# Windowed attention and two-layer MLP on one core: means of v per head pair in the first chunk, and a listed order for its first operations

## The chip, the cores and the metric

The kernel runs on one core of one Trainium2 chip. The metric is device time in microseconds, from the first to the last instruction with what lies around them; the median of three runs is given, and one execution was taken with a profile. TensorE multiplies matrices, VectorE and ScalarE work on 128 partitions side by side, GpSimd does a little of the same more slowly, and SyncE (SP) starts the transfers between HBM and the core's memory, SBUF.

## The reference

q, k and v are (4, 8, 768, 64): 4 batches, 8 heads, 768 positions, 64 features.

```python
k_sum = k.reshape(B, H, nb, 32, D).max(axis=3)
v_sum = v.reshape(B, H, nb, 32, D).mean(axis=3)
scores_l = scale * (q @ k.T), masked to |i - j| < 16
scores_s = scale * (q @ k_sum.T) + log(32)
a = exp(scores_all - max); a = a / (sum(a) + 1e-9)
out = a @ concat(v, v_sum)
h = x @ w_in                     # x: 3072 x 512, w_in: 512 x 2048
return maximum(0.01 * h, h) @ w_out
```

Every position sees its window of 31 neighbours and 24 block columns (maximum of k, mean of v over 32 positions). x is the attention output of all heads side by side. All is fp32.

## The kernel before, in words

The 3072 tokens are cut into 8 chunks of 384 (`NCH`), each with 4 head pairs (`NP`) and 3 tiles of 128 tokens to a pair: 12 units to a chunk (`UPC`). A unit's attention is this chain: scores on TensorE (`scores`, tiles s0 and s1 for the two heads), one VectorE operation that adds the mask, writes the result to e and its minimum to m (`lowest`), the exponential on ScalarE with its sum in z (`expo`), a guard (z + 1e-9), a reciprocal and the product e times 1/z on VectorE (`guard`, `rec`, `nrm`), a transpose on TensorE into t and its copy pt on ScalarE, the value product o on TensorE (`values`), and the copy of o into x on ScalarE with what the rounding left on VectorE (`xhi`, `xlo`). In the first chunk each unit does this on its own (`unit`); in the second, two units go together (`pair`, groups "g" in the names); later four.

A unit's 120 keys lie in one tile k: for each of 6 half tiles 96 window columns, copied from kn by ScalarE (`windows`), and 24 block columns, copied from ksum by VectorE (`k_s`); ksum is VectorE's maximum over kn (`k_max`). The values lie likewise in v: 96 rows per half tile from HBM, and 24 rows of means. For batch 0 the means come from TensorE: `v_mean_pe` loads all of v of batch 0 as three tiles of 512 KB (vb) and multiplies six pieces with a small averaging matrix that stands behind the mask, into 24 x 512 numbers; ScalarE copies these to vs0, and GpSimd copies them into the v tile of each of the four pairs.

The MLP takes a chunk's x in 16 blocks f of 128 hidden columns: 12 matmuls into h (three products of split numbers for four pieces of 128 features), an activation into gs and ghi on ScalarE, their difference glo on VectorE, and 9 matmuls into three accumulators a0 to a2. The first block's 12 matmuls are split in 9 and 3 (`CUT`), the 9 needing the units of three head pairs only. Its weights arrive as 512 KB tiles (w) of f 0, 1, ... for each of the two matrices and are split on the chip (`weights`): two steps on ScalarE, three on VectorE, of 512 columns each. Chunk 0 runs f 0 to 9, then chunk 1 all 16, then chunk 0 the rest; behind them the later batches go through a scheme with fewer multiplications, which the change does not touch.

What runs when is decided while the program is built. Every operation gets an engine, a cost and a due time (`prio`), and `Plan.order` lists them: the engine that is free first takes, of the operations that are ready by the planner's own clock, the one with the lowest due time. The `LOADS` list gives the first transfers in order. Every engine then executes its operations strictly in that order, and so does SP with the transfers. In gaps that the planner expects on TensorE it puts spare matmuls of zeros (L1343, tile `spare`) until the MLP has begun. Buffers are rings: q, k tiles have two (`KR`), v tiles three (`VR`), so the load of the fourth v tile waits for the first one's value products.

## Time and profile before

| | us |
|---|---|
| median of 3 runs (610.81 to 611.47) | 611.4 |
| span of the profiled execution | 610.0 |
| TensorE busy | 603.5 (99%) |
| VectorE busy | 470.8 (77%) |
| ScalarE busy | 351.2 (58%) |
| GpSimd busy | 4.5 (1%) |
| moved by DMA | 129.99 MB, 213 GB/s |

The span is what lies between the first and the last instruction; the median of the runs stands 1.4 us above it. A matmul's recorded end is modelled and overlaps the next one's start, so a busy TensorE isn't one at its peak, and the spare matmuls count as busy too; what an instruction costs in a dense queue is the distance between two starts. An idle time in brackets is that of the engine in front of the instruction, with what ended it.

### The profile page before, as it was taken

To read this page: it belongs to the slowest core of one execution; us is meant where nothing else is said; L and a number is where in the kernel's file an instruction comes from. 1 tells how busy PE (TensorE), PEld (TensorE's weight loads), DVE (VectorE), ACT (ScalarE), POOL (GpSimd) and SP (SyncE) were. 2 spreads that over 40 slices of the span, in tenths; PEclk is the share of its full clock that TensorE was granted. 3 is DMA by queue.
4 is the path that set the end of the run, shared out by engine and by line. 5 is a ranking of instruction groups with operands and counts; after the bars stand their busy time and mean duration, and the time that the engine had idled before them with its cause. 6 is when DMAs were issued, how large, how long until landed. Compare 5 with 4: busy or idle time off the path is not lost.

```text
span 610.0 us, 12907 instructions
## 1 busy us (share of the span) xinstructions
PE 603.5 (99%) x4676; PEld 539.8 (88%) x4676; DVE 470.8 (77%) x1281; ACT 351.2 (58%) x965; POOL 4.5 (1%) x10
## 2 busy tenths in 40 slices
PE   8999999999999999999999999999999999999997
PEld 6588889889988889989898897989889899999996
DVE  5899999964889995625688884777987874878787
ACT  5899996653766676505567565762816353516060
POOL 0200000000000000000000000000000000000000
PEclk9999999999999999999999999999999999999999
DMA  8897998896868826517498582975848384747552
GB/s 285 251 301 240 298 301 251 264 328 196 272 218 268 258 77 186 187 43 212 115 273 247 159 245 75 280 247 174 299 157 256 119 250 153 237 147 239 155 156 104
DMA packets 83358, 129.99 MB, mean 213 GB/s; under 512 B 7072, under 2 KB 51424, under 8 KB 83296
## 3 DMA queue, kind: packets, MB, share of 16 engines
q1 hardware_dynamic: 83296, 129.18, 68.1%
q8 instruction: 37, 0.61, 0.4%
q14 instruction: 25, 0.20, 0.1%
HBM read 97.72 MB, written 29.36 MB: 208 GB/s over the span
## 4 chain that ended last, share of the span: by engine, by line
PE 88%; DVE 6%; ACT 3%; DMA 1%; issue 1%; SPq 0%; DVEq 0%
PE L L1229 19%; PE h L724 12%; PE X L1090 7%; PE W L1090 7%; PE Z L1090 7%; PE B_a L1040 4%; PE a L744 4%; PE a L745 4%; PE a L743 4%; PE Y L1090 4%; PE B_s L1040 2%; ACT e L383 1%; PE B_to L1040 1%; PE vps L284 1%; DMA big<-in_k_dram 1%
## 5 line engine op out<-in xcount | busy, mean ns | idle before, releaser
L724 PE MATMUL h<-x,win_hi 128*128 128x384 f32 x320 | 82.7, 339 | 0.0
L383 ACT ACTIVATE e<-e,m 128x120 f32<-128x120 f32 x192 | 73.6, 387 | 4.0 <-DVE m L376 3.9
L1229 PE MATMUL L<-wout_hi,win_hi 128*128 128x512 f32 x168 | 66.5, 396 | 0.0
L1229 PE MATMUL L<-wout_hi,win_lo 128*128 128x512 f32 x168 | 65.7, 391 | 0.0
L1229 PE MATMUL L<-wout_lo,win_hi 128*128 128x512 f32 x168 | 65.6, 391 | 0.0
L724 PEld LDWEIGHTS h<-x,win_hi 128*128 128x128 f32 x320 | 57.7, 188 | 2.3 <-issue 0.2
L724 PE MATMUL h<-x,win_lo 128*128 128x384 f32 x160 | 53.8, 336 | 0.0
L743 PE MATMUL a<-wout_hi,ghi 128*128 128x512 f32 x120 | 48.4, 403 | 0.0
L745 PE MATMUL a<-wout_hi,glo 128*128 128x512 f32 x120 | 47.3, 394 | 0.0
L744 PE MATMUL a<-wout_lo,ghi 128*128 128x512 f32 x120 | 47.1, 392 | 0.1
L1229 PEld LDWEIGHTS L<-wout_hi,win_lo 128*128 128x128 f32 x168 | 31.5, 188 | 6.7
L1229 PEld LDWEIGHTS L<-wout_hi,win_hi 128*128 128x128 f32 x168 | 31.6, 188 | 5.8
L1229 PEld LDWEIGHTS L<-wout_lo,win_hi 128*128 128x128 f32 x168 | 31.6, 188 | 5.7
L383 ACT ACTIVATION_READ_ACCUMULATOR e<-e,m 128x1 f32 x192 | 36.4, 190 | 0.0
L734 DVE TENSOR_TENSOR glo<-gs,ghi 128x384 fp32r<-128x384 f32 x40 | 22.1, 554 | 17.1 <-ACT gs L728 16.4
L731 ACT ACTIVATE ghi<-h 128x384 fp32r<-128x384 f32 x40 | 19.4, 486 | 26.7 <-PE h L724 26.6
L1186 ACT COPY P<-X 128x384 f32<-128x384 f32 x19 | 9.0, 473 | 37.0 <-PE X L1090 36.9
L724 PEld LDWEIGHTS h<-x,win_lo 128*128 128x128 f32 x160 | 30.0, 188 | 0.0
L315 ACT COPY k<-big 128x288 f32<-128x288 f32 x64 | 24.7, 433 | 4.5 <-DMA big<-in_k_dram 4.5
L745 PEld LDWEIGHTS a<-wout_hi,glo 128*128 128x128 f32 x120 | 22.5, 188 | 5.4 <-DVE glo L734 0.4
L744 PEld LDWEIGHTS a<-wout_lo,ghi 128*128 128x128 f32 x120 | 22.6, 188 | 3.9 <-DVE wout_lo L693 0.4
L743 PEld LDWEIGHTS a<-wout_hi,ghi 128*128 128x128 f32 x120 | 22.6, 188 | 3.4
(630 smaller groups left out, 1626.0 us busy)
## 6 DMA issues: line engine op xcount, KB each, us to landing
win_hi<-sums SPq DMA_DIRECT2D x73, 256.0 KB
win_lo<-sums SPq DMA_DIRECT2D x71, 256.0 KB
big<-in_w_dram SPq DMA_DIRECT2D x32, 512.0 KB
sums<-big SPq DMA_DIRECT2D x32, 512.0 KB
v<-in_v_dram SPq DMA_DIRECT2D x32, 288.0 KB
big<-in_k_dram SPq DMA_DIRECT2D x16, 400.0 KB
k<-in_q_dram SPq DMA_DIRECT2D x32, 192.0 KB
wout_hi<-sums SPq DMA_DIRECT2D x21, 256.0 KB
```

What stands on the lines that cost most here:

```text
L315: nc.scalar.copy(k, x)
L383: nc.scalar.activation(out=e[:, n], in_=e[:, n], func=AF.Exp, scale=-1.0, bias=m[:, n:n + 1], accum_out=z[:, n:n + 1])
L724: nc.tensor.matmul(h[:, :T], w[:, 512 * f + 128 * k:512 * f + 128 * k + 128], x[:, T * k:T * k + T], start=n == 0, stop=n == 11)
L731: nc.scalar.activation(out=gnew(tag, G("ghi", f)), in_=tl[G("h", f)][:, :T], func=AF.Prelu, alpha=0.01)
L734: nc.vector.tensor_tensor(out=gnew(tag, G("glo", f)), in0=tl[G("gs", f)], in1=tl[G("ghi", f)].bitcast(F32), op=ALU.subtract)
L743: nc.tensor.matmul(o, gh, wout_hi[:, f], start=f == f0, stop=False)
L744: nc.tensor.matmul(o, gh, wout_lo[:, f], start=False, stop=False)
L745: nc.tensor.matmul(o, gl, wout_hi[:, f], start=False, stop=f == f1 - 1)
L1040: nc.tensor.matmul(o[:, x:x + 256], g, w[l], start=fresh and m == 0, stop=m == 5, skip_group_check=True)
L1090: nc.tensor.matmul(o[:, :T], w[:, l, 128 * k:128 * k + 128], x[y][:, T * k:T * k + T], start=start and n == 0, stop=n == 5, skip_group_che ...
L1186: nc.scalar.copy(tmp(K("P1")), ps("X"))
L1229: nc.tensor.matmul(o, g, w[:, f], start=s + m == 0, stop=s == 1 and m == 5)
```

## The change

In the first chunk the means of v are computed per head pair p. `v_mean_pe(p, ...)` makes the 24 x 128 means of one pair from 9 matmuls of 128 columns: six on the v tile of the pair, which is loaded anyway and holds the first half of the positions in overlapping bands (`band`), and three on a tile of 192 KB with the second half (`mm`). They go to partitions 96 to 119 of the bank that the spare matmuls use, which now write partitions 0 to 63. ScalarE copies 128 columns per pair; GpSimd copies into the v tile as before. In all tiles the block columns now stand behind the 96 window columns, and the scale of the scores is applied in the copies into the k tile. In the first chunk the guard is an activation with a bias on ScalarE, the product e times 1/z is one VectorE operation per head with a scalar per partition, and the block-max copies run on GpSimd. The k columns of pair 2 lie in a buffer of their own, so that its load needs no ring place. The order of 580 early operations is written out as a list (`FIRST`, numbers of the operations as they are made) that goes ahead of the due times; `LOADS` is listed anew, and due times and rates of the planner have other values.

```diff
+FIRST = [
+    1, 9, 0, 13, 12, 3, 26, 30, 2, 29, 10, 312, 11, 25, 5, 504, 43, 518, 505, ...
...
+        rank = {n: (-1000.0 + 0.001 * i, n) for i, n in enumerate(FIRST)}
...
-            o = min((x for x in cand[e] if x["ready"] <= t), key=lambda x: (x["prio"], x["n"]))
+            o = min((x for x in cand[e] if x["ready"] <= t), key=lambda x: rank.get(x["n"], (x["prio"], x["n"])))
...
-LOADS = [('kn', 0, 0), ('q', 0, 1), ('q', 0, 0), ('kn', 0, 1), ('mask',), ('vb', 0, 0), ...
+LOADS = [('kn', 0, 0), ('q', 0, 0), ('mask',), ('vb', 0, 0), ('v', 0, 0), ('kn', 0, 1), ...
...
-    def v_mean_pe(t):
-        def load(j):
-            x = bigs(("vb", 0, j))
-            nc.sync.dma_start(out=x.rearrange("p (t d) -> p t d", t=2), in_=a["v0"][j])
...
-            nc.tensor.matmul(tl["vps",][:NS], mask[:, 3 * LK + 20 - 4 * n:3 * LK + 44 - 4 * n], tl["vb", 0, j][:, 512 * i:512 * i + 512],
+    def v_mean_pe(p, t, ahead):
+        key, kv = ("vb", 0, p), ("v", 0, p)
+        half = NT // 2
+        def load():
+            nc.sync.dma_start(out=new("out", key, [128, 512], bufs=TPC)[:, :128 * half], in_=a["v0"][p])
+        def band(n):
+            nc.tensor.matmul(spare[96:LK, 128 * p:128 * p + 128], mask[:96, 3 * LK + 54 - 2 * n:3 * LK + 78 - 2 * n], tl[kv][:96, n], start=n == 0, stop=False)
+        def mm(n):
+            w = 3 * LK + 20 - 4 * (half + n)
+            nc.tensor.matmul(spare[96:LK, 128 * p:128 * p + 128], mask[:, w:w + NS], tl[key][:, 128 * n:128 * n + 128], start=False, stop=n == half - 1)
...
-            nc.scalar.copy(tl["vsum", 0], tl["vps",][:NS])
+            nc.scalar.copy(tl["vs0",][96:LK, 128 * p:128 * p + 128], spare[96:LK, 128 * p:128 * p + 128])
...
-            nc.scalar.copy(k, x)
+            nc.scalar.mul(k, x, -1.0 / math.sqrt(D))
...
-            nc.vector.tensor_copy(k, tl["ksum", b, p].unsqueeze(1).broadcast_to([128, 2 * TPC, NS]))
+            (nc.vector if c or not KSP else nc.gpsimd).tensor_scalar(out=k, in0=tl["ksum", b, p].unsqueeze(1).broadcast_to([128, 2 * TPC, NS]), scalar1=-1.0 / math.sqrt(D), scalar2=None, op0=ALU.mult)
...
         def guard():
             z = tiles_of(m)[2][:, part]
-            nc.vector.tensor_scalar(out=z, in0=z, scalar1=1e-9, scalar2=None, op0=ALU.add)
+            nc.scalar.activation(out=z, in_=z, func=AF.Identity, bias=tiny)
...
-            nc.vector.tensor_tensor(out=e[:, part], in0=e[:, part], in1=z[:, part].unsqueeze(2).broadcast_to([128, 2, LK]), op=ALU.mult)
+            nc.vector.tensor_scalar(out=e[:, n], in0=e[:, n], scalar1=z[:, n:n + 1], scalar2=None, op0=ALU.mult)
...
-                    nc.tensor.matmul(spare[:, :128], zero[:, :128], zero[:, :128], start=True, stop=True)
+                    nc.tensor.matmul(spare[:64, :128], zero[:, :64], zero[:, :128], start=True, stop=True)
```

How the queues stand. First SP's queue of transfers from its beginning, before; big holds kn, vb and w tiles, and in_v0 is the copy of v for the means:

```order
L244 DMA big_87<-in_k_dram 128x800
L310 DMA k_0_1_102<-in_q_dram 128x384
L310 DMA k_0_0_104<-in_q_dram 128x384
L244 DMA big_87<-in_k_dram 128x800
L230 DMA mask_78<-in_mask_dram 128x404
L278 DMA big_87<-in_v0_dram 128x1024
L244 DMA big_87<-in_k_dram 128x800
L278 DMA big_87<-in_v0_dram 128x1024
L310 DMA k_0_2_233<-in_q_dram 128x384
L278 DMA big_87<-in_v0_dram 128x1024
L244 DMA big_87<-in_k_dram 128x800
L672 DMA big_87<-in_w_dram 128x1024
```

And after:

```order
L278 DMA big_87<-in_k_dram 128x800
L361 DMA k_0_0_104<-in_q_dram 128x384
L264 DMA mask_78<-in_mask_dram 128x438
L314 DMA vb_0_0_107<-in_v0_dram 128x384
L370 DMA v_0_0_109<-in_v_dram 96x768
L278 DMA big_87<-in_k_dram 128x800
L361 DMA k_0_1_112<-in_q_dram 128x384
L314 DMA vb_0_1_114<-in_v0_dram 128x384
L370 DMA v_0_1_118<-in_v_dram 96x768
L728 DMA big_87<-in_w_dram 128x1024
L278 DMA big_87<-in_k_dram 128x800
L361 DMA k_0_2_174<-in_q_dram 128x384
```

Pair 0's q, mask, vb and v stand directly behind its kn, and the same four of pair 1 follow; w of f 0 moved from twelfth to tenth place, the first v from thirteenth to fifth.

TensorE's queue around the scores of units 6 to 8 (t is a transpose, vps the means, o a value product), before:

```order
L371 MATMUL s0_6_341<-k_0_2_233 64x120 x2
L371 MATMUL s1_6_342<-k_0_2_233 64x120 x2
L371 MATMUL s0_7_349<-k_0_2_233 64x120 x2
L371 MATMUL s1_7_350<-k_0_2_233 64x120 x2
L284 MATMUL vps_249<-big_87,mask_78 24x512
L371 MATMUL s0_8_369<-k_0_2_233 64x120 x2
L371 MATMUL s1_8_370<-k_0_2_233 64x120 x2
L284 MATMUL vps_249<-big_87,mask_78 24x512
L388 MATMUL t_4_387<-ident_77,e_2_300 120x128 x2
L284 MATMUL vps_249<-big_87,mask_78 24x512 x2
```

And after, where the means are written to spare:

```order
L448 MATMUL o_1_335<-pt_0_271,v_0_0_109 64x64 x4
L448 MATMUL o_0_343<-pt_0_271,v_0_0_109 64x64 x4
L442 MATMUL t_4_351<-ident_77,e_2_283 120x128 x2
L425 MATMUL s0_6_356<-big_87,k_0_2_174 64x120 x2
L425 MATMUL s1_6_357<-big_87,k_0_2_174 64x120 x2
L317 MATMUL spare_100<-v_0_2_191,mask_78 24x128
L425 MATMUL s0_7_372<-big_87,k_0_2_174 64x120 x2
L425 MATMUL s1_7_373<-big_87,k_0_2_174 64x120 x2
L317 MATMUL spare_100<-v_0_2_191,mask_78 24x128 x5
L321 MATMUL spare_100<-vb_0_2_186,mask_78 24x128 x2
L448 MATMUL o_2_401<-pt_1_315,v_0_0_109 64x64 x4
L321 MATMUL spare_100<-vb_0_2_186,mask_78 24x128
```

Three value products (o_1, o_0, o_2) stand ahead of or between these scores now; before, the first one, o_0, stands 59 rows behind the piece shown, with 29 spare matmuls between. In all, 103 spare matmuls stood between the first scores and the last part of h_0_0, and 52 stand there now.

ScalarE's queue around the first weight step (big 128x512, the tile of f 0), before:

```order
L383 ACTIVATE e_3_356,z_3_358<-e_3_356,m_3_357 128x120 x4
L684 ACTIVATE big_87<-big_87 128x512
L289 COPY vs0_399<-vps_249 24x512
L690 CAST win_hi_73<-big_87 128x512
L445 CAST x0_80<-o_0_435 128x128
L439 COPY pt_2_446<-t_4_387 120x256
L445 CAST x0_80<-o_1_440 128x128
L315 COPY k_0_3_297<-big_87 128x3x96 x2
L445 CAST x0_80<-o_2_456 128x128
```

And after (z is the guard):

```order
L474 ACTIVATE z_1_212<-z_1_212,tiny_98 128x2
L437 ACTIVATE e_2_283,z_2_285<-e_2_283,m_2_284 128x120
L740 ACTIVATE big_87<-big_87 128x512
L437 ACTIVATE e_2_283,z_2_285<-e_2_283,m_2_284 128x120
L326 COPY vs0_312<-spare_100 24x128
L474 ACTIVATE z_2_285<-z_2_285,tiny_98 128x2
L494 COPY pt_1_315<-t_2_302 120x256
L746 CAST win_hi_73<-big_87 128x512
L366 ACTIVATE big_87<-big_87 128x3x96
L494 COPY pt_1_315<-t_3_325 120x256
L366 ACTIVATE big_87<-big_87 128x3x96
L437 ACTIVATE e_2_283,z_2_285<-e_2_283,m_2_284 128x120
```

The weight step stands ahead of three of the four exponentials of units 4 and 5, where before it stood behind those of unit 7; the copies of the means, 24x128 instead of 24x512, follow it directly. Ahead of the last x cast of the chunk there stood 6 weight steps before, and 9 now.

## Rows read from the trace of the kernel before

**Rows 1.** Busy us of each engine by stretch (instructions), granted clock, DMA share, GB/s

```profile
0.00:8.00 8.00, 6.89 (x99) 6.46 (x99) 2.01 (x4) 2.76 (x5) 0.70 (x6) 1.00 0.77 250
8.00:16.00 8.00, 7.37 (x80) 4.10 (x81) 6.04 (x41) 6.25 (x28) 0.00 (x0) 1.00 0.94 326
16.00:24.00 8.00, 7.61 (x78) 3.73 (x76) 6.68 (x26) 5.57 (x20) 2.93 (x3) 1.00 0.89 206
60.00:80.00 20.00, 20.00 (x170) 17.20 (x170) 19.74 (x56) 18.99 (x49) 0.00 (x0) 1.00 0.91 296
```

**Rows 2.** Chain of waits behind 56 us: start us, us, what it ran on

```profile
57.65 2.11 PE h L724 x12
...
579.01 1.05 PE Z L1090 x6
```

**Rows 3.** Timeline of TensorE: start us, us, line, operation, tiles, count

```profile
5.90 0.64 PE L371 MATMUL s<-k 64*64 64x120 f32 x16
...
18.49 1.90 PE L284 MATMUL vps<-big,mask 128*24 128x512 f32 x4
20.32 1.79 PE L1343 MATMUL spare<-zero 128*128 128x128 bf16 x29
22.05 0.69 PE L394 MATMUL o<-pt,v 120*64 120x64 f32 x16
...
24.77 0.44 PE L371 MATMUL s<-k 64*64 64x120 f32 x8
25.13 0.45 PE L394 MATMUL o<-pt,v 120*64 120x64 f32 x8
25.51 0.43 PE L388 MATMUL t<-ident,e 128*120 128x128 f32 x2
25.88 0.45 PE L394 MATMUL o<-pt,v 120*64 120x64 f32 x8
...
34.91 0.63 PE L724 MATMUL h<-x,win_hi 128*128 128x384 f32 x2
...
53.38 0.32 PE L371 MATMUL s_('g', 9, 1)_943<-k 64*64 64x120 f32 x2
```

**Rows 4.** Timeline of ScalarE, first 41 us (in brackets idle us before, and releaser)

```profile
3.83 0.77 ACT L315 COPY k<-big 128x288 f32<-128x288 f32 x2 [1.81 <-DMA big<-in_k_dram]
...
19.77 0.70 ACT L684 ACTIVATE big<-big 128x512 f32<-128x512 f32 x1 [1.49 <-DMA big<-in_w_dram]
...
27.31 0.35 ACT L439 COPY pt<-t 120x256 f32<-120x256 f32 x1
27.56 0.44 ACT L315 COPY k<-big 128x288 f32<-128x288 f32 x1
27.89 0.27 ACT L445 CAST x<-o 128x128 fp32r<-128x128 f32 x1
28.05 0.41 ACT L383 ACTIVATE e<-e,m 128x120 f32<-128x120 f32 x1
28.34 0.20 ACT L383 ACTIVATION_READ_ACCUMULATOR e<-e,m 128x1 f32 x1
28.44 0.27 ACT L445 CAST x<-o 128x128 fp32r<-128x128 f32 x1
...
34.45 0.27 ACT L445 CAST x<-o 128x128 fp32r<-128x128 f32 x1
...
40.01 0.68 ACT L690 CAST win_hi<-big 128x512 fp32r<-128x512 f32 x1
40.60 0.70 ACT L684 ACTIVATE big<-big 128x512 f32<-128x512 f32 x1
```

**Rows 5.** Timelines of GpSimd and of VectorE, 21 to 35 us

```profile
21.06 2.93 POOL L327 COPY v<-vs 24x768 f32<-24x768 f32 x3 [19.76 <-ACT vs L289]
...
22.07 1.24 DVE L693 TENSOR_TENSOR win_lo<-big,win_hi 128x512 fp32r<-128x512 f32 x1 [0.75 <-ACT win_hi L690]
...
33.74 0.68 DVE L693 TENSOR_TENSOR win_lo<-big,win_hi 128x512 fp32r<-128x512 f32 x1
```

More of the change, by code (lines that the diff above doesn't have):

```diff
@@ L82, in __init__, with op @@
         self.ops, self.rings, self.users, self.slot = [], {}, {}, {}
-    def op(self, eng, cost, prio, fn, after=(), use=(), alloc=(), size=0, rate=250.0, port=False):
+    def op(self, eng, cost, prio, fn, after=(), use=(), alloc=(), size=0, rate=275.0, port=False):
         o = {"eng": eng, "cost": cost, "prio": prio, "fn": fn, "after": list(after), "size": size, "rate": rate, "n": len(self.ops)}
@@ L184, in build @@
     ident = cst.tile([128, 128], F32, name="ident")
-    mask = cst.tile([128, 3 * LK + 44], F32, name="mask")
+    mask = cst.tile([128, MW], F32, name="mask")
     def gap(n, src, tag):
@@ L201, in build @@
     make_identity(nc, ident)
+    zero = cst.tile([128, 128], BF16, name="zero")
+    nc.vector.memset(zero, 0.0)
+    tiny = cst.tile([128, 1], F32, name="tiny")
+    nc.vector.memset(tiny, 1e-9)
+    spare = ps_acc.tile([128, 512], F32, tag="a2", name="spare")
     def win(n, at, size):
@@ L247, in red @@
             x = tl["kn", b * CPB, p][:, WIN:WIN + S].rearrange("p (n r) -> p n r", r=BLK)
[L248 to L249 removed]
+            (nc.gpsimd if pooled else nc.vector).tensor_reduce(out=new("ksum", ("ksum", b, p), [128, NS], bufs=5), in_=x, axis=AX.X, op=ALU.max)
+        key, pooled = ("kn", b * CPB, p), b == 0 and p in KPOOL
         kn_op[key] = load_op(key, t - 1.3 - ahead, load, after=gate(b), alloc=[("big", key, 0)], size=128 * (S + 2 * WIN) * 4)
[L251 to L253 removed]
+        ksum_op[b, p] = P.op("POOL" if pooled else "DVE", POOL(S) if pooled else DVE(S), t, red, after=[kn_op[key]], use=[key], alloc=[("ksum", ("ksum", b, p), 5)])
+    vs_ops, vs_last = {b: [] for b in range(B)}, []
     def v_mean(b, j, t, ahead):
@@ new lines, in v_mean_pe @@
+    def v_mean_pe(p, t, ahead):
[8 more added lines that the diff above has]
+            nc.tensor.matmul(spare[96:LK, 128 * p:128 * p + 128], mask[:, w:w + NS], tl[key][:, 128 * n:128 * n + 128], start=False, stop=n == half - 1)
+        def copy():
+            if p == 0:
+                new("out", ("vs0",), [128, 512], bufs=TPC)
+            nc.scalar.copy(tl["vs0",][96:LK, 128 * p:128 * p + 128], spare[96:LK, 128 * p:128 * p + 128])
+        lv = v_op[0, p][0]
+        o = load_op(key, t - 1.5 - ahead, load, alloc=[("out", key, TPC)], size=128 * 128 * half * 4)
+        x = vs_last[:]
+        for n in range(2 * TPC):
+            y = P.op("PE", 225, t + 0.01 * n, lambda n=n: band(n), after=[lv, mask_op], use=[kv] + ([("vps",)] if p + n else []), alloc=[] if p + n else [("a2", ("vps",), 1)])
+            y["behind"], x = x and x[0], [y]
+        for n in range(half):
+            y = P.op("PE", 225, t + 0.1 + 0.01 * n, lambda n=n: mm(n), after=[o], use=[key, ("vps",)])
+            y["behind"], x = x[0], [y]
+        vs_last[:] = x
+        o = x[0]
+        vsum_op[0, p] = P.op("ACT", ACT(128, True), t + 0.1, copy, after=[o], use=[("vps",), ("vs0",)] if p else [("vps",)], alloc=[] if p else [("out", ("vs0",), TPC)])
@@ L1330, in build @@
         first[y]["behind"] = first[x]
-        first[y]["prio"] = first[x]["prio"] + 0.001
     todo = P.order()
-    zero = cst.tile([128, 128], BF16, name="zero")
-    nc.vector.memset(zero, 0.0)
-    spare = ps_acc.tile([128, 512], F32, tag="a2", name="spare")
     with tc.manual_schedule():
```

150 lines of the change are left out of this document (77 added, 73 removed), and 18 rows, old and new, of the table FIRST.

## Prediction

> **What bounds the kernel now.** I read the busy times by stretch first, then the chain of waits, then the timelines of TensorE and ScalarE. In the stretch from 60 to 80 us TensorE is busy for all 20.00 of 20 us [rows 1], and in the chain of waits one TensorE instruction follows the other from there until 580.06 us (the first and the last of these pieces are in [rows 2]). So the end is: the moment at which TensorE becomes gapless, plus a fixed amount of matmul work. What the change can move is that moment. It can be read at two places. At 34.91 us the three last matmuls of the first MLP block h_0_0 start, and from then on the queue is dense; at 53.38 us the scores of group 9 start [rows 3]. Between the two places stand 18.47 us, and the work in them is h_0_1 to h_0_4, three second-layer blocks, groups 7 and 8. The changed queue has the same blocks between the same two places in another order. So the question is when h_0_0's last part starts.
>
> It waits for the last x cast of the first chunk, on ScalarE at 34.45 us [rows 4]. ScalarE is late because it stood idle earlier. By the end of this cast it has done 21.7 us of work (summed below) since its first window copy at 3.83 us, and 34.60 - 3.83 - 21.7 = 9.1 us were idle. Where they are: ScalarE is busy for only 2.76, 6.25 and 5.57 us of the first three 8 us [rows 1]; the weights of f 0 arrive at 19.77 us after 1.49 us of waiting, and no value product runs before 22.05 us [rows 3, 4], since the means of v need three loads of 512 KB and six matmuls first, and only then do the four GpSimd copies run [rows 5]. TensorE fills that time with spare matmuls (29 in one row of [rows 3]).
>
> **The change part by part.** *Loads.* Up to the fourth v tile the old list carries 4 kn (410 KB each), 4 q (197), mask (207), 3 vb (524), one w (524) and 4 v (295), 5.9 MB; the new one has 4 vb of 197 KB, together 5.1 MB. More important is the order: q, k and v of head pair 0 come as a set, then pair 1, then w of f 0 as the tenth load, 2.94 MB into the list. By the rates of [rows 1] 2.00 MB have moved by 8 us and 0.326 MB/us follow, so w lands at 10.9 us if loads finish strictly in their order. In the trace it doesn't: the same w was 4.53 MB into the old list and landed at 19.77 us, when 2.00 + 2.61 + 3.77 x 0.206 = 5.39 MB had moved. With that 0.86 MB of lag it lands at 13.5 us. I take 13.0, since the row at hand is this very load, and keep 10.9 to 13.5.
>
> *ScalarE.* Prices are distances between starts in [rows 4]: exponential with its accumulator read 0.39 (28.05 to 28.44), window copy 0.33, pt copy 0.25, x cast 0.16, a weight step of 512 columns 0.59. Before, up to the last x cast: 24 exponentials 9.36, 10 windows 3.3, 12 pt 3.0, 12 x 1.92, 6 weight steps 3.54, the copy of the means about 0.59: 21.7 us. After: the same exponentials, windows, pt and x 17.6, 9 weight steps that now stand ahead of the last x 5.31, four narrow copies of the means at an x cast's 0.16, 0.64, and 12 guards. A guard on 2 elements isn't in this trace on ScalarE. Below it lies the accumulator read, one element, 0.10; above it the exponential less that read, 0.29 for 120 elements. I take 0.15, nearer the read since it has hardly any elements: 1.8 us, bounds 1.2 to 3.5. Sum 25.3 us.
>
> The Trainium skill, "ScalarE: Activation LUTs", section "Rules for kernel authors", speaks against this move: it wants adds on VectorE and budgets about 0.3 us for each ACTIVATE. By that the guards would take 0.15 us more each; eight of them stand behind the wait for w, so the time would be 1.2 us more than what I forecast below. The x cast of 128 elements at 0.16 us [rows 4] says less.
>
> *The new end of ScalarE's part.* Ahead of the weight step that waits for w, its queue has 9 exponentials, 4 windows, 2 pt and 4 guards, 5.9 us; behind it up to the last x 25.3 - 5.9 = 19.4 us. What stands behind is no longer starved: the value products of pair 0 need only v and vb of pair 0, which land before w. So the last cast ends at 13.0 + 19.4 = 32.4 us, and with 0.3 us of gaps at 32.7. Its start stood 0.46 us ahead of h_0_0's last part before; that gives 33.0 us, against 34.91.
>
> *TensorE's own sum* must fit too. The means take 36 matmuls of 128 columns in place of 6 of 512 (0.95 us each in [rows 3], four in 1.90 with two records to a matmul, so 5.5 to 5.8 in all). For 128 columns a quarter is 0.24, and a transpose, which has 128 columns as well, takes 0.18 (0.37 a pair); I take 0.21, 7.6 us, bounds 6.5 to 8.6. Prices from [rows 3]: scores 0.36, values 0.38, transposes 0.37 a unit. Start 5.5 (5.90 before, with fewer spares ahead), 12 units 13.3, means 7.6, scores of group 6 twice a unit's 0.7, nine of twelve matmuls of h_0_0 1.6 (2.11 for twelve, [rows 2]), 52 spares behind the first scores at 1.79/29 = 0.062, 3.2: 31.9 us without any wait. It lies 1.1 us under ScalarE's 33.0, so that much of its waiting is free, and 33.0 stays. The means cost 2 us more of TensorE, hidden in what were spares (103 behind the first scores before, 52 now); if that cover were gone they would cost those 2 us.
>
> *VectorE* gives away 12 guards and the four block-max copies, and its broadcast product becomes two products with a scalar. It was busy 2.01, 6.04 and 6.68 us of the first three 8 us [rows 1], so its saving alone is worth nothing there. *GpSimd* has eight operations instead of four; each wide copy takes 0.98 us (2.93 for three, [rows 5]). The block-max copy, 144 elements instead of 768, is between 0.18 by size and 0.98; I take 0.3. It stands ahead of the scores of its pair, but a mean copy can stand ahead of it in that queue, and then the scores wait up to 1 us.
>
> *Behind it.* The blocks up to group 9 take 18.47 us as before, so scores of group 9 start at 51.5 instead of 53.38. By the last x ScalarE has done three weight steps more than before and VectorE five by its queue, so neither starts the dense part behind. The sum: 34.91 - 33.0 = 1.9 us. The profiled span of 610.0 becomes 608.1; the runs' median of 611.4 lies 1.4 above the span, so I say **609.5 us**.
>
> **The rivals.** *More than that*: w lands at 10.9 and the guards take 0.10. ScalarE would be done at 10.9 + 19.0 = 29.9, and TensorE's 31.9 plus a little is what holds: 32.2, 608.7; with matmuls at 0.18 as well 1.1 us less, 607.6. Against it: the lag that w showed.
>
> *Not faster, the port*: GpSimd's operations lock VectorE out. While GpSimd copied from 21.06 us on, a subtraction of two SBUF tiles took 1.24 us, against 0.68 for the same at 33.74 [rows 5]. Four operations more, and in a stretch with more VectorE work, could put 1 to 2 us on the path through the normalisation and the transposes: 610.5 to 611.5. For it: the scores wait for GpSimd and VectorE in turn. Against it: VectorE has some 9 us idle in the first 24 us. The Trainium skill, "SBUF — State Buffer", section "SBUF: two separate sides", calls the pair of ports an exclusive lock for the whole instruction; row 22.07 agrees. By that rule eight operations of 0.3 to 0.98 us are 5.1 us in which such VectorE work stands, against 3.9 before.
>
> *Slower, ScalarE's queue*: it is the engine that gets more work, and it executes in order. If a guard costs the 0.39 of a whole exponential with its read, the eight behind w cost 1.9 us more, which just eats the gain: 611.4. If w lands 2 us after 13.0 besides, because v and q move at the 0.206 MB/us of the third row of [rows 1], everything behind it waits: 33.0 + 1.9 + 2.0 = 36.9, 2.0 later than before, 613.4. With cheap guards the gain is gone from w at 14.9 on, with dear ones from 13.0 on. For it: ScalarE has no other idle time to give. Against it: the lag that this takes is twice what the row of w shows.
>
> *TensorE's clock*: it is 1.00 in every row of [rows 1], with a queue full of spares. With half of these, and waits for loads between 7 and 16 us, it could fall to the lower of the two levels, 1.2 GHz. Some 5 us of matmuls there would take 10; less the 1.1 us that are free this is 3.9 us on the path, 613.4, or 610.9 if only half of the stretch is hit.
>
> *Nothing of it done*: that the first value products don't come earlier is excluded by the queue: they stand ahead of the scores of unit 6 now, behind those of unit 8 before.
>
> **How the numbers follow.** Forecast (a gain of 1.2 to 3 us) 0.48; more than that 0.10; port, no difference 0.20; ScalarE's queue 0.12, of it 0.07 slower by over 0.2% and 0.05 same; clock 0.10, half slower and half same. What a measurement of this kernel can tell from no change is 0.2%, 1.2 us: faster means below 610.2, slower above 612.6. Faster 0.58, same 0.30, slower 0.12. The range reaches from a little below the far end of the gain, 607.2, to 612.6; beyond it lie most of the slower cases and a sliver of the large gains.
>
> **What the profile will show.** Right: the first value products at about 15 us instead of 22.05; w of f 0 at 12 to 14 us and ScalarE hardly idle from there; the last x cast ends at 32 to 33.5; scores of group 9 at 51 to 52; no idle TensorE behind. A guard at a distance of 0.10 to 0.2. Wrong would be: ScalarE idle again behind 14 us (then GpSimd or a load holds the scores), subtractions of over 1 us on VectorE in many rows, a granted clock under 1.00, or TensorE waiting for weights behind 35 us, so that the early start is given back before group 9.

## The result, and the profile after

| | before | after |
|---|---|---|
| median of four runs beside each other (us) | 611.28 (610.81 to 611.47) | 614.85 (614.5 to 616.07) |
| profiled execution: span (time) | 610.0 (611.4, median) | 612.9 (615.0) |
| scores of group 9 start | 53.38 | 54.76 |
| from there to the end of the span | 556.6 | 558.1 |

The ratio is 1.0060, with an interval of 1.0046 to 1.0075: the changed kernel is 3.6 us slower. The forecast was 609.5 us, 1.9 faster. Of the 2.9 us in the span 1.4 arise before group 9 and 1.5 behind it, where the prediction had put a fixed amount of work. What lies around the span is 2.1 us after; before it was 1.4 by the prediction's median, and 1.8 in a later run of the same kernel (611.46 against 609.7).

Busy time by stretch, after (columns as in [rows 1], with GpSimd's time ahead of the clock):

```profile
0.00:8.00 8.00, 6.35 (x73) 5.70 (x73) 2.41 (x15) 3.40 (x10) 1.25 (x7) 1.00 0.78 223
8.00:16.00 8.00, 7.30 (x76) 5.28 (x76) 5.59 (x24) 6.25 (x27) 1.21 (x2) 1.00 1.05 309
16.00:24.00 8.00, 7.54 (x105) 4.92 (x109) 6.39 (x37) 7.84 (x33) 3.05 (x5) 1.00 0.62 181
36.00:60.00 24.00, 24.00 (x197) 21.02 (x196) 23.36 (x75) 23.80 (x68) 0.00 (x0) 1.00 0.92 281
```

ScalarE, the fourth engine column, is busy for 7.84 of 8 us from 16 to 24 (5.57 before, [rows 1]). From 36 to 60 it is nearly full, 23.80 of 24, and VectorE has 23.36; in the kernel before that stretch reads:

```profile
36.00:60.00 24.00, 23.93 (x189) 20.39 (x188) 22.92 (x73) 22.78 (x66) 0.00 (x0) 1.00 0.84 259
```

TensorE's timeline, after (columns as in [rows 3], the counterpart of these lines):

```profile
5.69 0.64 PE L425 MATMUL s<-k 64*64 64x120 f32 x16
...
8.34 1.47 PE L317 MATMUL spare<-v,mask 96*24 96x128 f32 x12 [1.02 <-DMA v<-in_v_dram]
9.64 0.82 PE L321 MATMUL spare<-vb,mask 128*24 128x128 f32 x6
...
16.56 0.63 PE L448 MATMUL o<-pt,v 120*64 120x64 f32 x15
...
25.71 1.49 PE L317 MATMUL spare<-v,mask 96*24 96x128 f32 x12 [0.19 <-DMA v<-in_v_dram]
...
33.44 0.69 PE L448 MATMUL o<-pt,v 120*64 120x64 f32 x16
34.06 0.61 PE L780 MATMUL h<-x,win_hi 128*128 128x384 f32 x2
...
35.83 0.63 PE L1393 MATMUL spare<-zero 128*64 128x128 bf16 x8
36.40 0.62 PE L780 MATMUL h<-x,win_hi 128*128 128x384 f32 x2
...
54.76 0.32 PE L425 MATMUL s_('g', 9, 1)_938<-k 64*64 64x120 f32 x2
```

The first value products do come early, at about 16.5 us instead of 22.05, but 5.5 us of lead have become 1.5 us of lag at h_0_0's last part: 36.40 against 34.91. The first nine matmuls of h_0_0, at 34.06, stand behind the last value product. In the kernel before they started here, ahead of the value products of the last two units:

```profile
30.70 0.60 PE L724 MATMUL h<-x,win_hi 128*128 128x384 f32 x2
```

ScalarE after (the counterpart of [rows 4]; z is a guard, vs a narrow copy of the means):

```profile
11.80 0.37 ACT L494 COPY pt<-t 120x256 f32<-120x256 f32 x1 [1.53 <-PE t L442]
...
13.35 0.30 ACT L474 ACTIVATE z<-z,tiny 128x2 f32<-128x2 f32 x1
13.54 0.38 ACT L437 ACTIVATE e<-e,m 128x120 f32<-128x120 f32 x1
...
13.92 0.66 ACT L740 ACTIVATE big<-big 128x512 f32<-128x512 f32 x1
...
34.60 0.48 ACT L500 CAST x<-o 128x128 fp32r<-128x128 f32 x2
```

The idle time of 1.53 us ahead of 11.80 is the last big one: between 11.80 and 34.60 ScalarE stands idle for 0.42 us in all. So the last x cast, the second of the two in row 34.60 (it starts at 34.75), is now set by how much ScalarE has to do. What ended the last long wait was a transpose, behind the means of the first pair on TensorE (rows 8.34 and 9.64), and not the load of w: no instruction waited for w, and its first step stood in the queue until 13.92. The guard at 13.35 is followed at 13.54, 0.19 later.

VectorE and GpSimd after (the counterpart of [rows 5]):

```profile
34.23 0.69 DVE L749 TENSOR_TENSOR wout_lo<-big,wout_hi 128x512 fp32r<-128x512 f32 x1
...
35.25 0.28 DVE L503 TENSOR_TENSOR x<-o,x 128x128 fp32r<-128x128 f32 x1
...
35.98 0.28 DVE L503 TENSOR_TENSOR x<-o,x 128x128 fp32r<-128x128 f32 x1
```

```profile
10.32 0.59 POOL L382 TENSOR_SCALAR k<-ksum 128x144 f32<-128x144 f32 x1 [4.76 <-DVE z L478]
```

The last two x subtractions come at 35.25 and 35.98, behind a weight subtraction and reductions of group 6, the second behind a weight step too; before, they came at 34.35 and 34.74.

### The profile page after: what moved, and what is told of

Its sections match the earlier page's. It is cut to its first block, busy times and chain, and to the rows that moved or that the text cites. A ratio compares the mean times of both kernels' runs of the same rounds, so it can differ in the third digit from the quotient of the medians.

```text
span 612.9 us, 12938 instructions
## 1 busy us (share of the span) xinstructions
PE 605.0 (99%) x4667; PEld 542.4 (88%) x4667; DVE 469.5 (77%) x1278; ACT 353.6 (58%) x980; POOL 6.7 (1%) x14
## 4 chain that ended last, share of the span: by engine, by line
PE 82%; ACT 7%; DVE 5%; DMA 4%; issue 1%; SPq 0%; DVEq 0%; ACTq 0%
PE L L1285 19%; PE h L780 9%; PE Z L1146 8%; PE W L1146 7%; PE X L1146 7%; PE B_a L1096 5%; PE Y L1146 4%; PE a L799 3%; PE a L800 3%; PE a L801 3%; PE B_s L1096 2%; ACT e L437 2%; DMA big<-in_k_dram 2%; PE B_to L1096 1%; ACT big L740 1%; DMA big<-in_w_dram 1%
## 5 line engine op out<-in xcount | busy, mean ns | idle before, releaser
L1194 ACT ACTIVATE win_hi<-U 128x384 fp32r<-128x384 f32 x28 | 14.6, 521 | 26.9 <-DVE U L1182 26.9
L366 ACT ACTIVATE k<-big 128x288 f32<-128x288 f32 x62 | 24.2, 438 | 6.5 <-DMA big<-in_k_dram 6.5
```

The costliest lines, as they stand in the source:

```text
L366: nc.scalar.mul(k, x, -1.0 / math.sqrt(D))
L1194: nc.scalar.activation(out=hi, in_=ps("X") if direct else tl[kt], func=AF.Prelu, alpha=0.01)
```

## Experiments

Four explanations were to be told apart: ScalarE has too much work (guards, copies); the order of TensorE and VectorE around h_0_0 is worse; something changed the matmuls behind group 9; the port or the clock. "g9" below is the start of the scores of group 9 and "rest" what follows it in the span; before they are 53.38 and 556.6, after 54.76 and 558.1. Ratios are to the kernel before on the same chip, whose medians lay between 611.38 and 611.49.

### Behind group 9: where a tile begins in its partition

Second-layer matmuls from 100 to 240 us, before and after (count, busy us, mean ns of one, idle us):

```profile
L744 PE MATMUL a<-wout_lo,ghi 128*128 128x512 f32 x82 | 32.0, 391 | 0.0
```

```profile
L800 PE MATMUL a<-wout_lo,ghi 128*128 128x512 f32 x84 | 33.2, 395 | 0.0
```

Nobody waits here, and the same matmul is 4 ns longer; the distance between two starts is 233.5 ns instead of 229.5. The kernel has 360 second-layer matmuls of this kind, the last of them at 239 us, and 360 x 0.004 = 1.4 us (an upper estimate, since not each shows it). ghi and glo are the 128 x 128 operand that is loaded ahead of such a matmul; the 512 columns that stream through are weights (wout). The change did not touch this code, but it moved these tiles: they began 64 bytes past a multiple of 512 within a partition, and now begin 288 past one, 224 further. The edits below show what that is made of. The longer mask tile moved the x tiles by 128, from 128 to 256 past (the x padding that a_gx takes back), and all behind them with it; the padding constant of ghi grew by 64 (160 to 224); and 32 are the place of the new one-float tile `tiny` with the guard's constant (b_guard, which adds that tile alone, takes 32 off the padding to keep ghi in its place).

**a_g0** takes the padding of ghi and glo back to that place, **a_gx** that of x too; **b_g384** gives the kernel before the place of after, 288, and **b_g128** another, 32.

```diff
# after, in a_g0 and in a_gx
-XGAP, GGAP = (416, 448, 384, 256), (224, 0, 0, 0)
+XGAP, GGAP = (416, 448, 384, 256), (0, 0, 0, 0)
+XGAP, GGAP = (288, 448, 384, 256), (128, 0, 0, 0)
# before, first number of GGAP in b_g384 and in b_g128
-GGAP = (416, 448, 384, 256), (160, 0, 0, 0)
+GGAP = (416, 448, 384, 256), (384, 0, 0, 0)
+GGAP = (416, 448, 384, 256), (128, 0, 0, 0)
```

> The changed kernel with one constant set back in effect: the pad ahead of the ghi tiles is 0 bytes instead of 224, so that ghi and glo begin 64 bytes past a multiple of 512 within a partition, as in the kernel before (in the changed kernel they begin 288 past one). The order of the instructions is that of the changed kernel. Theory A (the pace of the second matmul, a<-wout,ghi, hangs on where ghi lies): from 100 to 240 us the pitch of one a matmul falls from 233.5 ns to the 229.5 ns of before, 360 of them make 1.4 us, the scores of group 9 stay at 54.8 us, and the time is 613.5 us (changed kernel: 614.85). Rival B (the pace is set by what runs beside it, or is chance): pitch 233.5 ns and 614.85 us, as in the changed kernel.

> The changed kernel with the pads set so that ghi and glo (pad 128 instead of 224) and the x tiles (first pad 288 instead of 416) all begin at the byte offsets of the kernel before. The order of the instructions is that of the changed kernel. Theory A: pitch of an a matmul 229.5 ns, of an h matmul 174.5 ns instead of 175.3 (480 of them: 0.4 us), so 613.1 us, 0.4 us below the run with ghi alone moved. Rival: x has no part in it, the same time as the run with ghi alone moved, or 614.85 us if neither has.

> The kernel before with its ghi and glo tiles moved the other way: pad 384 instead of 160, so that they begin 288 bytes past a multiple of 512, as in the changed kernel. Nothing else differs. Theory A: the pitch of an a matmul rises from 229.5 to 233.5 ns and the time by 1.4 us, to 612.7 us. Rival B: 611.3 us, no change.

> The kernel before with its ghi and glo tiles 32 bytes lower: pad 128 instead of 160, so that they begin 32 bytes past a multiple of 512 (and of 64) instead of 64. Nothing else differs. Theory A64 (what counts is whether the tile begins at a multiple of 64 bytes): the pitch of an a matmul rises from 229.5 to 233.5 ns, as at 288, and the time to 612.6 us. Rival A512 (it is the place 288 itself): 229.5 ns and 611.5 us.

| | median (range) | ratio (interval) | g9 | rest |
|---|---|---|---|---|
| a_g0 | 614.21 (613.59 to 615.28) | 1.0047 (1.0034 to 1.0060) | 55.03 | 557.1 |
| a_gx | 614.06 (613.11 to 616.83) | 1.0048 (1.0029 to 1.0067) | 56.86 | 556.6 |
| b_g384 | 612.68 (612.09 to 613.40) | 1.0018 (1.0010 to 1.0027) | 53.14 | 557.9 |
| b_g128 | 612.50 (612.12 to 613.35) | 1.0017 (1.0008 to 1.0026) | 53.54 | 557.8 |

The same group of matmuls, in the order a_g0, a_gx, b_g384, b_g128:

```profile
L800 PE MATMUL a<-wout_lo,ghi 128*128 128x512 f32 x84 | 33.0, 392 | 0.0
```

```profile
L800 PE MATMUL a<-wout_lo,ghi 128*128 128x512 f32 x86 | 33.6, 391 | 0.0
```

```profile
L744 PE MATMUL a<-wout_lo,ghi 128*128 128x512 f32 x82 | 32.6, 397 | 0.0
```

```profile
L744 PE MATMUL a<-wout_lo,ghi 128*128 128x512 f32 x83 | 33.0, 397 | 0.0
```

One number in the kernel before costs it 0.18% (1.1 us) and brings the longer matmul; the same number in the changed kernel takes it away. Both 288 and 32 lie 32 past a multiple of 64 and are dear; 64 is cheap, and no other place was run. Of the 224 bytes, 128 and 64 are multiples of 64; it is the 32 of the guard's constant that take the tiles off one. So about 1.1 of the 1.5 us are put down to the place of ghi and glo: two runs of the kernel before show that price in their medians. In the changed kernel the trace shows it (rest 558.1 to 557.1), while the median falls by 0.6 us, under its forecast of 1.4, with intervals that overlap (1.0046 to 1.0075 and 1.0034 to 1.0060). The last 0.4 fit the x tiles (rest 557.1 in a_g0, 556.6 in a_gx), but that is one trace each, and the medians, 614.21 and 614.06, don't tell them apart: open.

### The order around h_0_0

**a_x** moves the last x casts and subtractions ahead of a weight step, a weight subtraction and two reductions. **a_nofirst** is a_gx without the list.

```diff
# after; moves: operation, operation that it is put behind
-    todo = P.order()
+    todo = P.order(); at = {o["n"]: o for o in todo}; [(todo.remove(at[n]), todo.insert(todo.index(at[to]) + 1, at[n])) for n, to in ((338, 670), (656, 669), ...
# a_gx, in a_nofirst
-        rank = {n: (-1000.0 + 0.001 * i, n) for i, n in enumerate(FIRST)}
+        rank = {}
```

> The changed kernel with the x of the last two units ahead of weight work: on ScalarE their two casts stand ahead of one weight step (0.58 us), on VectorE their two subtractions stand ahead of one weight subtraction and two score reductions. Theory C (h_0_0's last part waits for the subtractions at 35.25 and 35.98 us): the casts end at 34.4 and the subtractions at 34.8, the last part starts at 35.2 instead of 36.40, the scores of group 9 at 53.6 instead of 54.76, and the time is 613.7 us (changed kernel: 614.85). Rival D: the weights that were put back are late in their turn, TensorE waits as long for the next block, and the time stays within 0.3 us of 614.85.

> The changed kernel with ghi, glo and x at the byte offsets of the kernel before, without the listed order of the early operations: the planner's own order by due times takes its place, also further on. Theory F (the list pays for itself): the last x cast and the start of TensorE's dense stretch come 1 to 3 us later, the time is 614 to 617 us against 613.3 for the same kernel with the list. Rival N (the list is what spoils the change, by putting eleven weight steps ahead of the last cast): dense at 34.9 us or sooner, 611.8 us.

a_x: 615.77 (614.61 to 618.32), 1.0076 (1.0057 to 1.0096). The casts came at 34.22 and the subtractions were done by about 35.0, yet TensorE shows:

```profile
34.23 0.63 PE L780 MATMUL h<-x,win_hi 128*128 128x384 f32 x2
...
36.58 0.62 PE L780 MATMUL h<-x,win_hi 128*128 128x384 f32 x2
```

x was ready 1.6 us before it was used. The theory that the late x alone holds the last part falls: nine matmuls (1.6 us) and eight spare ones (0.57) stand between the last value product and this part. a_nofirst: 614.64 (613.75 to 616.69), 1.0061 (1.0042 to 1.0080), beside a_gx's 614.06. The planner's own order puts the nine at 30.59, as in the kernel before; the last part still comes at 36.54, though here the scores and transposes of group 7 stand ahead of it, from 35.56 on, and TensorE waits 1.2 us for gs of ScalarE behind it. The list by itself is worth nothing that these medians can tell.

### The work on ScalarE and GpSimd

**a_guard** puts the guards back on VectorE, **a_ks** the block-max copies; **b_guard** gives the kernel before the guards on ScalarE, with the place of ghi kept.

```diff
# after, in a_guard (b_guard is the reverse, in the kernel before)
-            nc.scalar.activation(out=z, in_=z, func=AF.Identity, bias=tiny)
+            nc.vector.tensor_scalar(out=z, in0=z, scalar1=1e-9, scalar2=None, op0=ALU.add)
# after, in a_ks
-            (nc.vector if c or not KSP else nc.gpsimd).tensor_scalar(out=k, ...
+            nc.vector.tensor_scalar(out=k, ...
```

> The changed kernel with the 12 guards of the first chunk back on VectorE, at the same places of the listed order; nothing else moves. Theory S (ScalarE's queue, without a gap from 12 us on, sets when the last x cast ends): 12 x 0.207 us = 2.5 us leave it, VectorE takes 12 x 0.09 to 0.16 us, the last two casts start at 32.4 instead of 34.60 us, h_0_0's first nine at 32.2 instead of 34.06, its last part at 34.5 instead of 36.40, the scores of group 9 at 52.9 instead of 54.76, and the time is 613.0 us (changed kernel: 614.85). Rival V (the late load of the last v tile or VectorE sets it): the last cast within 0.5 us of 34.6 and the time within 0.4 us of 614.85. A third outcome is a loss: the guard's trip to VectorE makes each unit longer, 615.5 us.

> The changed kernel with the four block-max copies of the first chunk on VectorE instead of GpSimd, at the same places of the listed order; nothing else moves. A copy took 0.57 to 0.63 us on GpSimd and takes 0.14 to 0.23 us on VectorE. Theory S: each pair's first scores come some 0.4 us sooner, ScalarE's queue starts sooner by as much (its first gap of 1.94 us ends with the first scores), the rest is as before: 614.5 us. Rival P (GpSimd's copies and wide copies hold up VectorE at a shared port): VectorE's instructions of 16 to 22 us, 0.31 us for a scaling beside a wide copy, fall to the 0.19 us of the rest, and the time falls by 1 us or more, to 613.8.

> The kernel before with the 12 guards of the first chunk on ScalarE instead of VectorE, at the same places of the order, ghi and glo at the offsets they had. Theory S: ScalarE has idle time until the first weight lands (19.77 us) and hardly any behind it, so that of the 12 guards of 0.207 us some 6 push its queue: the last x cast starts 1.2 us later, at 35.65 instead of 34.45, h_0_0's last part at 36.1 instead of 34.91, and the time is 612.7 us (kernel before: 611.45). Rival: the guard's place on ScalarE saves VectorE as much and shortens each unit by the trip between the engines, 611.2 us.

a_guard: 615.05 (613.49 to 616.46), 1.0052 (1.0040 to 1.0064). a_ks: 615.74 (614.28 to 616.74), 1.0070 (1.0058 to 1.0082). Both profiled executions, and that of a_gx, met the low clock of the next part, so these three compare with each other: h_0_0's last part at 38.62 in a_gx, 38.61 in a_ks, 37.92 in a_guard. The block-max copies on GpSimd cost nothing that shows here; the guards cost 0.7 us in these traces. The median of a_guard tells no gain: 615.05 instead of the 613.0 forecast, beside 614.85 for the changed kernel, which by its time alone is the rival's outcome. And one trace is a coarse measure: after, a_g0 and a_gxw, all at clock 1.00 with the same order up to h_0_0, have the last part at 36.40, 36.76 and 36.82. A difference of 0.4 us or less between two traces says nothing; the guards are tried again below. b_guard: 611.73 (611.49 to 612.99), 1.0010 (1.0002 to 1.0019), under its forecast of 612.7. There ScalarE has 7.30 us of idle time up to the last cast; 5.46 are left with the guards, and the last part stays where it was:

```profile
34.77 0.66 PE L726 MATMUL h<-x,win_hi 128*128 128x384 f32 x2
```

So the same twelve guards are nearly free where ScalarE has idle time; what they cost where it has none is under "Together".

**a_w** puts two weight steps and the exponentials of group 6 behind the last x casts; **a_v4** gives the v tiles a fourth buffer, so that no load waits for a value product (its bytes come out of the padding, with ghi at 64). In both, the planner listed all that follows anew.

```diff
# after, in a_w
-    todo = P.order()
+    [P.ops[n].update(behind=P.ops[670]) for n in (332, 338, 674, 676, 678, 680)]; todo = P.order()
# after, in a_v4
-KR, VR, PTR, ER = 2, 3, 2, 2
+KR, VR, PTR, ER = 2, 4, 2, 2
```

> The changed kernel with the weight steps of the second block of f1 and the first of f2, and the exps of group 6, put behind the casts of the last two units on ScalarE; the order behind is worked out anew by the same rules, so that some rows further on stand elsewhere too. Theory S: three weight steps of 0.57 us less stand ahead of the last cast, which starts at 32.9 instead of 34.60 us; h_0_0's last part, behind its first nine, starts at 34.9 instead of 36.40, the scores of group 9 at 53.3, and the time is 613.4 us (changed kernel: 614.85). Rival D (what was put back is late in its turn): TensorE waits for the exps of group 6 or for the weights of f1 between 37 and 50 us, and the time is 614.8 us.

> The changed kernel with four buffers for the v tiles instead of three, so that the load of the fourth doesn't wait for the first value product; the bytes come out of the pads (x pads 288, 192, 0, 0 and ghi pad 0, so ghi begins 64 past a multiple of 512, as in the kernel before). The load goes out at about 14 us instead of 21.45, so the means of the last pair are no longer late. Theory S (ScalarE's queue is the bound): TensorE's wait at 25.71 us goes, but the last x cast starts within 0.5 us of 34.6, h_0_0's last part within 0.5 us of 36.40, and the time is 613.6 us, all of the 1.2 us from the address of ghi. Rival V (the last v tile is the bound): the load lands 4 us sooner, h_0_0's last part is at 34.5 us, the scores of group 9 at 52.9 us, and the time is 611.7 us.

a_w: 621.65 (619.18 to 622.75), 1.0161 (1.0142 to 1.0179). The last part came at 38.04, under a_gx's 38.62 at the same clock, and then TensorE waited behind it, as in these rows:

```profile
42.57 0.62 PE L442 MATMUL to_('g', 7, 1)_722<-ident,e 128*120 128x128 f32 x4 [0.44 <-DVE e L578]
...
60.21 0.44 PE L780 MATMUL h<-x,win_lo 128*128 128x384 f32 x1 [0.43 <-DVE win_lo L749]
```

What is put off here is wanted at once there. a_v4: 617.37 (616.17 to 619.14), 1.0097 (1.0083 to 1.0110), with the last part at 37.12 and new waits of TensorE for pt (1.6 us, at 87) and for ghi (1.1 us, at 105) in its other order. It tells nothing of the v load; that stays untested.

### The clock

In some executions of the changed kernel's variants TensorE's granted clock drops. Windows of 1 us in a_gx, then the same stretch of after:

```profile
8.00:9.00 1.00, 0.08 (x1) 0.11 (x2) 0.17 (x1) 1.00 (x7) 0.00 (x0) 1.00 0.99 339
...
10.00:11.00 1.00, 1.00 (x6) 0.80 (x5) 1.00 (x5) 0.53 (x2) 0.28 (x1) 0.50 1.08 237
```

```profile
8.00:9.00 1.00, 0.66 (x7) 0.66 (x8) 0.17 (x1) 1.00 (x6) 0.00 (x0) 1.00 1.07 374
...
10.00:11.00 1.00, 1.00 (x17) 0.69 (x14) 1.00 (x7) 0.27 (x1) 0.59 (x1) 1.00 1.04 253
```

In a_gx the first product on the v tile came 0.58 us later, at 8.92; TensorE waited for the tile with nothing to run, and then worked at 0.50, 1.2 GHz, from 9.1 to 12.5 us: 6 records of matmuls from 10 to 11 us where after has 17. In a_ks, at the same low clock, the six and the three means of pair 0 read:

```profile
8.91 2.44 PE L317 MATMUL spare<-v,mask 96*24 96x128 f32 x12 [1.38 <-DMA v<-in_v_dram]
11.13 1.49 PE L321 MATMUL spare<-vb,mask 128*24 128x128 f32 x6
```

The means of this one pair take 3.6 us instead of 2.05, and h_0_0's last part comes 2.2 us later (38.62 against 36.40). **a_gxw** is a_gx with 16 spare matmuls in this wait.

```diff
# a_gx, in a_gxw
         def band(n):
+            [nc.tensor.matmul(spare[:64, :128], zero[:, :64], zero[:, :128], start=True, stop=True) for _ in range(16) if n + p == 0]
```

> The changed kernel with ghi, glo and x at the byte offsets of the kernel before (the one whose executions came out between 613.1 and 616.8 us) and with 16 empty matmuls put into TensorE's wait for the first v tile, 7.3 to 8.9 us. Theory K (that wait lets TensorE's clock fall to 0.50 from 9.4 to 12.6 us in some executions, which costs 2.2 us of the start, as the traces with and without it show): the granted clock stays at 1.00 in all executions, the first pt copy on ScalarE stands at 11.8 us, and the times lie between 613.0 and 613.8 us with a median of 613.3. Rival L (the spread comes from when the loads land): the times still spread over 2 us or more, up to 615.5.

a_gxw: 614.49 (614.16 to 615.84), 1.0054 (1.0042 to 1.0067). The clock was 1.00 in this stretch, here and in the three kernels below, which have the same filling; the last part came at 36.82 and g9 at 55.05. The fall is a cost of some executions and not the main one: three executions of a_gx lay between 613.1 and 613.4, with mean clocks of 0.998 to 1.000 (0.997 in the one shown). All five of a_gxw, at 0.999 to 1.000, lie above these three; whether the 16 matmuls cost something themselves wasn't tried. The median stayed 1.2 us over its forecast of 613.3; 0.77 of that is a wait in the profiled execution, for which no other run was made:

```profile
118.88 0.61 PE L781 MATMUL h<-x,win_hi 128*128 128x384 f32 x2 [0.77 <-ACT ghi L788]
```

### Together

Three kernels on top of a_gxw: **a_gwg** with the guards on VectorE, **a_gwx** with the order near h_0_0 by hand (the nine ahead of the last unit's transposes, no spare matmuls ahead of the last part, x operations ahead of weight steps), **a_all** with both.

```diff
# a_gxw, in a_gwx and a_all
-    todo = P.order()
+    todo = P.order(); at = ... for n, to in ((629, 628), (1258, 629), (326, 1258), (643, 642), (338, 670), ...
```

> The changed kernel with ghi, glo and x at the offsets of the kernel before and 16 empty matmuls in TensorE's first wait (614.5 us as measured), and the 12 guards back on VectorE. Theory S (ScalarE's queue): it loses 2.5 us of work but then waits about 0.9 us more for others, as the disturbed trace of the guard run showed (0.7 us gained): last x cast at 34.1 us, h_0_0's last part at 36.0 instead of 36.82, group 9 at 54.3 instead of 55.05, time 613.7 us. Rival: nothing, 614.5 us, the 0.7 us came from another cause.

> The same base kernel (614.5 us as measured), the guards left on ScalarE, with the order near h_0_0 changed by hand: its first nine matmuls stand ahead of the last unit's transposes on TensorE, in the place of the empty matmuls, none stand ahead of its last part, and the x casts and subtractions of the last four units stand ahead of weight steps on ScalarE and VectorE. Theory Q (what comes late is the order of the queues, the first nine behind the last value product and the empty matmuls behind them, not the amount of work): first nine at 31.5 us instead of 34.49, last part at 35.3 instead of 36.82, group 9 at 53.6 instead of 55.05, time 613.0 us. Rival D (the weights put back come late): TensorE waits for win_lo or wout_lo between 36 and 50 us and group 9 stays at 55 us, 614.5 us.

> Both edits together on the same base (guards on VectorE and the order near h_0_0 by hand). If S and Q add up: last part at 34.6 us, group 9 at 52.9, time 612.3 us. If they are the same 0.7 to 1.5 us twice: 613.0 us. If neither holds: 614.5 us.

| | median (range) | ratio (interval) | last part of h_0_0 | g9 |
|---|---|---|---|---|
| a_gxw | 614.49 (614.16 to 615.84) | 1.0054 (1.0042 to 1.0067) | 36.82 | 55.05 |
| a_gwg | 613.52 (612.06 to 614.85) | 1.0033 (1.0021 to 1.0045) | 35.71 | 53.94 |
| a_gwx | 614.97 (613.91 to 616.92) | 1.0067 (1.0052 to 1.0083) | 35.45 | 54.05 |
| a_all | 614.29 (613.70 to 615.29) | 1.0049 (1.0037 to 1.0061) | 34.73 | 53.68 |

a_gwg moves everything by the same 1.1 us, and nothing is given back: its rest is 556.3. The medians are 1.0 apart (0.8 forecast), but their intervals touch (1.0021 to 1.0045 and 1.0042 to 1.0067), and the execution that the trace shows is the fastest of its five, 612.06. So about 1 us for the guards is likely, and not sharply measured. a_gwx and a_all come earlier to h_0_0 and to group 9, and then TensorE waits. In a_gwx:

```profile
57.17 0.45 PE L781 MATMUL h<-x,win_lo 128*128 128x384 f32 x1 [0.74 <-DVE win_lo L750]
```

and in a_all:

```profile
56.14 0.62 PE L443 MATMUL to_('g', 9, 1)_933<-ident,e 128*120 128x128 f32 x4 [1.20 <-DVE e L579]
...
57.86 0.44 PE L781 MATMUL h<-x,win_lo 128*128 128x384 f32 x1 [0.74 <-DVE win_lo L750]
```

TensorE's queue can be brought forward by 2 us, and finds the weights and the exponentials of the second chunk not ready. These come from ScalarE and VectorE, but the sum of their work doesn't account for the waits. At 58 us both the kernel before and a_all have begun the sixth first-layer block; up to there ScalarE has done 23 weight steps before and 27 in a_all, VectorE 33 and 39. More is done, and the piece that is wanted isn't among it. In a_all VectorE reads:

```profile
56.51 0.69 DVE L750 TENSOR_TENSOR wout_lo<-big,wout_hi 128x512 fp32r<-128x512 f32 x1
57.11 1.29 DVE L750 TENSOR_TENSOR win_lo<-big,win_hi 128x512 fp32r<-128x512 f32 x2
```

The first of the two at 57.11 is the win_lo that TensorE waits for, the sixth, and it stands behind six subtractions of wout_lo. In the kernel before it stood behind three:

```profile
54.16 0.69 DVE L693 TENSOR_TENSOR win_lo<-big,win_hi 128x512 fp32r<-128x512 f32 x1
```

The e of group 9 (row 56.14) is late in the same way: its reciprocal, at 54.94, stands behind a wout_lo and another weight step on VectorE. So the order in which weights are split is the nearer reason for these waits. No run changed it, and whether another order would keep the 2 us is open. No version was faster than the kernel before.

## Why the prediction was wrong

**What held.** TensorE stays gapless behind, and the stretch between the two places was right: 18.36 us against the 18.47 forecast. The first value products came at about 16.5 (about 15 expected), the first weight step at 13.92 with w there already (w at 13.0), the means at 2.05 us for a pair against 7.6 / 4 = 1.9, the weight steps at 5.2 us against 5.31. The port rival fell: with GpSimd writing from 16.33 to 16.90, two products of VectorE that started at 16.34 were followed 0.48 us later; no VectorE row beside a GpSimd operation in the trace after is longer by more than about 0.2 us, and a_ks gained nothing. The Trainium skill, "SBUF — State Buffer", section "SBUF: two separate sides", has the lock for VectorE operations in a two-port mode or with two SBUF inputs. The subtraction at 22.07 in [rows 5] has two; whether these products use a two-port mode no run here shows, so they don't test that rule.

**First step that failed: ScalarE's sum.** It named the right engine, and the sum was 1.7 us short:

| up to the last x cast | forecast | measured |
|---|---|---|
| 24 exponentials | 9.36 | 9.58 |
| 10 windows | 3.3 | 3.69 |
| 12 pt, 12 x | 4.92 | 5.03 |
| 9 weight steps | 5.31 | 5.2 |
| 4 narrow copies | 0.64 | 1.04 |
| 12 guards | 1.8 | 2.49 |
| sum | 25.3 | 27.0 |

A guard takes 0.207, not 0.15, and a narrow copy 0.26, not 0.16: a nearly empty operation was priced too near its elements. The Trainium skill's 0.3 us for each ACTIVATE ("ScalarE: Activation LUTs", section "Rules for kernel authors") makes an estimate of 3.6 us for the guards, more than the 2.49 here: a guard's own duration is 0.28 to 0.30, the distance to the next start 0.207. That section's advice to keep adds on VectorE agrees with a_gwg, 1.0 us by the medians. The wait was another one, too: the forecast let the queue stand until w lands, but nothing waited for w. The last long wait, to 11.80, was for the transposes behind the first means, and from there ScalarE had 2.1 us of work ahead of w's step. With that step 0.9 later, behind which 21.0 us follow instead of 19.4 with 0.3 of gaps, the last cast starts at 34.75 in place of the 32.5 that the forecast means: 2.2 us.

**Second: from the cast to the last part**, 0.46 us was carried over from the kernel before; it is 1.65. The nine matmuls of h_0_0 had been counted in TensorE's sum, but as work that lies anywhere. They had moved behind the last value product, where they and eight spare matmuls stand on the path; and the x subtractions had moved behind a weight subtraction. "31.9 us without any wait" was a sum over the queue, and says nothing of what stands behind the last wait. Both orders could be read before any run. Together 3.4 us: 33.0 forecast, 36.40 measured.

**Third: "fixed work behind".** It was 1.5 us more, of it about 1.1 from where ghi and glo begin in a partition: the longer mask, the padding constant and the guard's one-float tile moved them by 224 bytes. All three were in the diff and got no price.

The rest adds up: 3.4 - 0.1 + 1.5 makes 4.8 us in the span (608.1 to 612.9), and 0.7 lie around it, 0.3 if the later run of the kernel before is taken; why, is open, as is the spread of 2 to 4 us among the executions of the changed variants, beyond those with a low clock. ScalarE's queue was the rival whose mechanism came true, by 27 us of work that leave it no slack behind 11.80 us, not by a late w nor by guards at 0.39; the clock rival came true in some executions only.

**Where the gain went.** Measured as distances between starts, ScalarE had 23.5 us of work up to the last cast before, and 7.3 us of idle time (not 21.7 and 9.1: the prices of a dense queue were too low for one with gaps). The earlier loads removed 3.4 of the 7.3, and 3.6 us of work were added: 2.49 of guards, 1.5 of weight steps, 0.5 of copies of the means, less 0.9 by which pt copies and x casts are cheaper in the dense queue. So the last cast starts at 34.75 against 34.45, nearly level, and the order behind it makes 1.2 of the 1.5 us of loss at h_0_0. Mending guards or order brings this back by 1 to 2 us in the traces (a_gwg, a_gwx, a_all). Where the order was changed, TensorE then waits for ScalarE and VectorE until 58 us, which have little time left (23.80 and 23.36 of 24 us in the trace after) and have other weights ahead of the ones wanted. a_gwg gives nothing back in its trace, and its median is still 2.1 us above the kernel before; that part is open.

## What to carry to other kernels

When idle time is taken out of an engine, sum up what is left for it to do to the end of the stretch that it feeds, and don't give it more work in the same change. A start that is read at one instruction needs the list of what stands on the other engines between the last wait and that instruction, in the new order. And a tile that is added or changes its size, be it one float, moves the tiles behind it: read the mean time of the unchanged matmuls in the dense part before the cause is looked for in the part that was edited.

## What the runs showed of the hardware

A matmul of 512 columns whose loaded operand (the 128 x 128 piece of ghi) began 32 bytes past a multiple of 64 within each partition, at 32 or 288, took 395 to 397 ns in the trace against 391 to 392 at 64, and 1.1 us in all for some 360 of them; the load itself took 188 ns at either place. An activation on two elements per partition cost ScalarE 0.19 to 0.21 us from start to start, a copy of 24 x 128 numbers 0.26. And the length of TensorE's wait for the first v tile does not tell by itself whether the clock falls. Waits of 0.99 us (a_guard, to 8.91), 1.04 (a_w, to 8.76), 1.35 (a_gx, to 8.92) and 1.38 (a_ks, to 8.91) were followed by a granted clock of 0.50 until 12.1 to 12.7 us; waits of 0.91 us (a_v4, to 8.79), 1.02 (after, to 8.34) and 1.03 (a_g0, to 8.68) were not. With 16 spare matmuls in the wait the clock was 1.00 in each of the four traces that had them.
